# An mLSTM cell in sub-chunks of 64 tokens, and a new order of the first chunk's steps

## The chip, the cores and the metric

The kernel runs on one core of one Trainium2 chip. The metric is the device time of one execution in microseconds (us). Three timed runs of the kernel before gave 483.16, 483.56 and 483.63; the median is 483.56. A core has five engines with a queue of instructions each, executed in the order of the program: PE (TensorE, the matrix products), DVE (VectorE), ACT (ScalarE), POOL (GpSimd) and SP (SyncE, which here only issues DMAs). An instruction waits at the head of its queue until what it reads is there and what it overwrites has been read; nothing behind it on that engine starts before. PE's weight loads (PEld in the profile) run ahead of its products.

## The reference

The first half is an mLSTM cell over q, k, v of 4 batches, 8 heads, 768 tokens and 40 features, with gates per token:

```python
for t in range(S):
    m_new = np.maximum(f_gate[:, :, t] + m, i_gate[:, :, t])
    f_stab = np.exp(f_gate[:, :, t] + m - m_new)
    i_stab = np.exp(i_gate[:, :, t] - m_new)
    m = m_new
    C = f_stab * C + i_stab * outer(vt, kt)      # 40 x 40 per head
    n = f_stab * n + i_stab * kt
    h_tilde = C @ qt
    y[:, :, t] = sigmoid(o_gate[:, :, t]) * h_tilde / max(abs(n . qt), 1)
```

The second half is a feed-forward block on y, seen as 3072 tokens of 320 features: `gelu(y @ w_in) @ w_out`, with w_in 320x2048 and w_out 2048x320, both given in 64-bit floats.

## The kernel before, in words

**Chunks.** The 768 tokens are cut into six chunks (c = 0 to 5) of 128 tokens. A chunk of all four batches is 512 tokens for the feed-forward block. Inside a chunk the recurrence is written as products: the scores `k q^T` times a matrix of weights W (an exp of gate sums, masked so that a token sees only earlier ones), times the values; plus what q reads from the state that the chunk began with (`far`, scaled by gT). After that the state (40 by 41 for each head; column 41 is n) is decayed by `dec` and grown by `k^T (v * ewT)`.

**Cell steps.** Class `Cell` has a method for each step. The order of the work is written out by hand in two strings, FRONT and DOWN; each letter is a step and `play` emits the instructions of all engines for the letters in that order. Small letters in FRONT are chunk 0's cell, capital ones chunk 1's: m/M mask on POOL (`mask`, L407), w/W weights (`weights`: eight exps on ACT for a batch, L433; for chunk 0 PE writes the gate sums into PSUM first, L428 and L430), g/G sigmoid of the output gate on ACT (L439), t/T turning q and k on PE (L482, with two copies on ACT, L485), s/S scores (`scores`, L508, a product with W on DVE), c/C `carry` (state products on PE, L546, the read of the state, L551, and the state's update on DVE), v/V values (`values`, L622), y/Y `finish` (five operations on DVE, L635 to L640), x/X turning y on PE (L657, copied by ACT into first_x or x_hi), R splitting x on DVE (L675, L676). From chunk 2 on the batches go in pairs: `scores_two` (L524), `read_two` (L579), `update_two` (L590), and the second batch of each pair has the two halves of its 128 tokens swapped when loaded, so that all four 64 by 64 quarters of the PE array can be used at once.

**The front.** Chunk 0's cell needs the gates' running sums and maxima on DVE (L252 to L259, for chunk 0, chunk 1 by E, chunks 2 to 5 by N) and their exps on ACT. Beside it the weights are converted from 64-bit bits in 26 pieces: ten of w_in (512 elements a partition; two pieces of 128 rows for every 256 columns of a half, and one that holds the remaining 64 rows for 512 of them) and sixteen of w_out (320 elements). The letter P or the step J fetches a piece into one of four buffers. The letter K (`conv_one`) is for the next piece: two operations on DVE (L358, L363), two on ACT that make its power of two (L360, L361), and one on DVE (L365). The letter J (`conv_two`) is for the next piece not yet finished: two on DVE (L372, L375), the first of which needs ACT's power; then it fetches the piece four further on. So piece n is ready after the n-th J.

The chunk 0 feed-forward runs in plain f32. A is an up-step on the first half of the 512 tokens, U on the second; there are four of each, and the k-th uses two pieces of w_in with the one of remaining rows: the first needs pieces 1 to 3, the second 4 and 5, the third 6 to 8, the fourth 9 and 10. Two that follow each other (`U U`) are put out as one. Each issues its products on PE (L762, L768) and then its two gelus on ACT (L772). F is one of sixteen rows of the down product (L869, 8 instructions on PE), each with its own piece of w_out. While chunk 0's feed-forward runs, chunk 1's cell is computed.

**The later stages.** For c = 1 to 5, `up` gives chunk c's up-projection in split precision (L817, L828, gelus L832), then the string DOWN mixes chunk c's down-projection (14 products, letter F, L892) with the cell of chunk c+1.

**Queues.** SP issues all loads and stores in program order. Its loads of q, k, v and the gates for a batch are issued as one DMA each, or two where the halves are swapped. M, the running maxima, goes to memory and is read back spread over all partitions (L178).

Of the kernel before, what the change touches and what calls it, by code (L numbers as in the profile page):

```python
# [16 lines left out]
P = 128  # L17
# [11 lines left out]
    I2 O0 g0 L0 P0 L1 E k1 t0 P1 P2 k7 w0 N k2 w1 O1 K L2 Q s0 O3 w2 q D k2 d P3 t1 w3 c0 L3 J v0 t2 K K y0 s1 I7 v1  # L29
    I8 O2 J g1 L4 I5 c1 K I1 I2 y1 s2 x0 t3 B4 O4 B5 g2 J x1 s3 v2 c2 L5 y2 H T0 x2 G0 v3 g3 c3 K y3 M1 J L6 J A x3  # L30
    M0 K W0 O7 K A O6 O5 J M2 W1 S0 C0 K J J T1 U U K L7 V0 K T2 r J J A G2 K G1 Y0 W2 S1 K M3 C1 A J S2 J K W3 K V1 C2
    Y1 T3 J J U U S3 V2 K K J G3 J Y2 C3 X0 K V3 J K F J F K K B8 F J K F F J K F F F R0 X1 J J K F J F K X2 F J K F
    J Y3 K F R1 J F Z B9 B10 F X3 R2 Z R3 F p"""
DOWN = """
    M0 Z M1 W0 F L3 F B3 W1 Z Z S0 K2 C0 F h0 M2 G0 G1 G2 G3 V0 V1 W2 F Q2 K3 Q3 Y0 M3 D3 F F N W3 F S2 F C2 h2 V2 V3 j F Y1
    X0 R0 Y2 F F X1 Z Y3 R1 F X2 R2 F X3 R3 F"""
# [3 lines left out]
def kernel(  # L40
# [35 lines left out]
    NW = 3  # L76
# [25 lines left out]
    ewT = const.tile([P, NCH - 1, BH], F32, name="ewT")  # L102
    gT = const.tile([P, NCH - 1, BH], F32, name="gT")
    dec = const.tile([P, NCH - 1, B * NP], F32, name="dec")
    state = [const.tile([P, NP, 2 * D1], F32, name=f"state{b}") for b in range(B)]
# [6 lines left out]
    W = {n: shared([P, H, L], F32, f"W{n}") for n in range(B - 1)}  # L112
# [6 lines left out]
    last = gates.tile([P, P], F32, name="last")  # L119
    eye = gates.tile([P, P], BF16, name="eye")  # L120
    beyond = gates.tile([P, L], BF16, name="beyond")
    f_sb = gates.tile([BH, NCH, L], F32, name="f_sb")
    i_sb = gates.tile([BH, NCH, L], F32, name="i_sb")
    M_d = dram.tile([NCH - 1, BH, L], F32, name="M_d")
    swapped_d = [dram.tile([P, n, BH], F32, name=f"swapped{n}") for n in (NCH - 2, NCH - 3)]
# [5 lines left out]
    quarters = tuple(slice(R // 2 * n, R // 2 * (n + 1)) for n in range(4))  # L131

    def swapped(c, b):

        return c > 1 and b % 2 == 1

    def load(n, first=0, end=4):

        if n >= NCH * B:
            return  # L140
        c, b = divmod(n, B)
        for src, dst in ((q, qb), (k, kb), (v, vb), (o_gate, None))[first:end]:
            if dst and swapped(c, b):
                x, to = src[b, :, c * L:(c + 1) * L, :].rearrange("h p d -> p h d"), dst[turn_of(n)][:, :, 0:D]
                for i in range(2):
                    nc.sync.dma_start(out=to[halves[i]], in_=x[halves[1 - i]])
                continue
            nc.sync.dma_start(out=dst[turn_of(n)][:, :, 0:D] if dst else out_of(n),
                              in_=src[b, :, c * L:(c + 1) * L, :].rearrange("h p d -> p h d"))
# [17 lines left out]
    def load_M(n, to=None):  # L167

        if not B <= n < NCH * B:
            return  # L170
        c, b = divmod(n, B)
        src = M_d[c - 1, b * H:(b + 1) * H, :]
        if to is not None:
            Mb[n] = to
            nc.sync.dma_start(out=to, in_=src.unsqueeze(0).to_broadcast([P, H, L]))
            return
        Mb[n] = shared([P, H, L], F32, "W") if n // 2 == NW else wts.tile([P, H, L], F32, name="W", tag="W")
        nc.sync.dma_start(out=Mb[n].rearrange("p h l -> p (h l)"),  # L178
                      in_=src.rearrange("h l -> (h l)").unsqueeze(0).to_broadcast([P, H * L]))
# [8 lines left out]
    nc.gpsimd.memset(last, 0.0)  # L188
# [6 lines left out]
    for t in state:  # L195
        nc.gpsimd.memset(t, 0.0)
# [196 lines left out]
    class Cell:  # L393
# [16 lines left out]
        def weights(self, b):  # L410
# [23 lines left out]
            if n in (B, B + 1):  # L434
                load_M(n + 2)
# [579 lines left out]
```

## Time and profile before

| | |
|---|---|
| median of three timed runs | 483.56 us |
| span of the profiled execution | 487.5 us |
| its own time beside the span | none given beyond the span; it is 3.9 us over the median |
| PE busy | 474.4 us, 97% of the span |
| DVE, ACT, POOL busy | 351.2, 222.7, 72.0 us |
| first up-step of chunk 0 on PE (L762) | starts at 44.24 us |
| first product of chunk 1's feed-forward (L817) | starts at 133.4 us in the chain that ended last |
| first product of chunk 2's and of chunk 3's | 206.8 and 279.5 us |
| mean granted TensorE clock | 0.986 |

A row of the timeline gives start, duration, engine, line, operation, and out<-in by the program's tile names; f32 products appear as two records each. Products are pipelined, so the time that one group costs PE is read from its start to the start of the next group, not from the durations, which overlap. In brackets stands how long the engine was idle before the row and what ended that. "Busy" on PE is therefore an upper reading.

### The profile page before, as it was taken

The numbers are of one execution on the slowest core, as the hardware profiler recorded it, in microseconds if no ns is written. First come the engines' busy times: TensorE is split into PE (matmuls) and PEld (weight loads), VectorE is DVE, ScalarE is ACT, GpSimd is POOL, SyncE is SP. The second block draws the span as 40 slices with busy tenths as digits, with TensorE's granted clock in tenths as the row PEclk, the third lists the DMA queues.
The fourth block names the chain that finished last, engine by engine and source line by source line (L and its number), as shares of the span: only waits on it lengthen the run. The fifth ranks groups of instructions, "written<-read, shape, count | busy, mean of one in ns | idle before, by whom it ended". The sixth has DMA issues, their size and how long they took to land.

```text
span 487.5 us, 13234 instructions
## 1 busy us (share of the span) xinstructions
PE 474.4 (97%) x5380; PEld 411.0 (84%) x5380; DVE 351.2 (72%) x762; ACT 222.7 (46%) x477; POOL 72.0 (15%) x104
## 2 busy tenths in 40 slices
PE   8999999999999999999999999989999999999997
PEld 7787788877777898977898977889987898977997
DVE  7699879798879979855599756569755599724321
ACT  6786999954433852104852103852104672113300
POOL 3002120000020125400234200213300024000000
PEclk9699999999999999999999999989999999999999
DMA  9997986268431239551356541355561241000001
GB/s 175 193 171 172 199 194 148 69 168 204 125 59 13 34 71 192 83 111 14 41 107 162 79 103 16 37 94 127 108 123 19 30 78 24 28 28 0 1 1 54
DMA packets 170428, 44.57 MB, mean 91 GB/s; under 512 B 156448, under 2 KB 163904, under 8 KB 170368
## 3 DMA queue, kind: packets, MB, share of 16 engines
q1 hardware_dynamic: 170368, 43.73, 45.5%
q8 instruction: 42, 0.69, 0.6%
q14 instruction: 18, 0.15, 0.1%
HBM read 39.58 MB, written 4.13 MB: 90 GB/s over the span
## 4 chain that ended last, share of the span: by engine, by line
PE 70%; issue 13%; DVE 9%; POOL 2%; ACT 2%; SPq 2%; DMA 1%; DVEq 0%; POOLq 0%; ACTq 0%
PE po L892 23%; PE pu L817 16%; PE po L869 7%; PE pu L762 5%; PE pu L828 4%; PE ph L622 3%; PE ps L508 2%; SPq L158 1%; PE pu L768 1%; PE px L657 1%; PE ps L524 1%; PE pt L482 1%; POOL g L407 1%; DMA g<-M_d 1%; PE pf L590 1%
## 5 line engine op out<-in xcount | busy, mean ns | idle before, releaser
L892 PE MATMUL po<-w_out,g 128*128 128x160 f32 x640 | 91.6, 300 | 0.0
L892 PEld LDWEIGHTS po<-w_out,g 128*128 128x128 f32 x640 | 87.7, 190 | 2.1 <-ACT g L832 1.8
L832 ACT ACTIVATE g<-pu 128x512 f32<-128x512 f32 x80 | 40.8, 614 | 53.0 <-PE pu L828 52.8
L892 PE MATMUL po<-w_sums,sums 128*128 128x160 f32 x320 | 49.9, 310 | 1.9 <-issue 1.9
L892 PEld LDWEIGHTS po<-w_sums,sums 128*128 128x128 f32 x320 | 45.9, 196 | 3.1 <-issue 2.4
L817 PE MATMUL pu<-x_hi,w_in_hi 128*128 128x512 f32 x160 | 41.7, 402 | 0.0
L817 PE MATMUL pu<-x_lo,w_in_lo 128*128 128x512 f32 x160 | 40.6, 395 | 0.0
L667 ACT ACTIVATE x_hi<-px 128x384 fp32r<-128x384 f32 x20 | 9.8, 489 | 67.3 <-PE px L657 67.3
L433 ACT ACTIVATE W<-W,aT 128x128 f32<-128x128 f32 x128 | 39.2, 390 | 0.1
L817 PEld LDWEIGHTS pu<-x_hi,w_in_hi 128*128 128x128 f32 x160 | 28.5, 188 | 9.3 <-ACT g L832 4.1
L817 PEld LDWEIGHTS pu<-x_lo,w_in_lo 128*128 128x128 f32 x160 | 30.1, 188 | 7.2
L749 DVE TENSOR_TENSOR sums<-g 128x512 f32<-128x512 f32 x20 | 13.7, 687 | 30.8 <-ACT g L832 30.8
L869 PE MATMUL po<-w_out,g 128*128 128x320 f32 x128 | 35.2, 433 | 0.0
L869 PEld LDWEIGHTS po<-w_out,g 128*128 128x128 f32 x128 | 24.0, 190 | 9.6
L817 PE MATMUL pu<-x_all,w_mid 128*128 128x512 f32 x80 | 31.6, 395 | 0.0
L832 ACT ACT_TABLE_LOAD x5 | 6.4, 1283 | 55.1 <-PE pu L828 41.3
L817 PE MATMUL pu<-x_all,w_in_mid 128*128 128x512 f32 x80 | 31.6, 395 | 0.0
L721 DVE TENSOR_TENSOR w_in_mid<-w_in_hi,w_in_lo 128x512 fp32r<-128x512 f32 x20 | 13.8, 688 | 24.4 <-PE pu L817 24.4
L905 DVE TENSOR_TENSOR o_sb<-po,o_sb 128x320 f32<-128x320 f32 (+1 forms) x27 | 12.5, 463 | 25.7 <-PE po L892 21.7
L445 POOL MEMSET g<- 32x1024 f32 x8 | 7.6, 945 | 151.2 <-ACT W L433 125.6
L762 PE MATMUL pu<-first_x,w_in 128*128 128x256 f32 x128 | 29.2, 382 | 0.6 <-DVE w_in L375 0.6
L407 POOL TENSOR_SCALAR_AFFINE_SELECT W<-W 128x1024 f32<-128x1024 f32 (+2 forms) x20 | 20.9, 1056 | 59.6 <-DMA W<-M_d 51.6
(183 smaller groups left out, 915.5 us busy)
## 6 DMA issues: line engine op xcount, KB each, us to landing
W<-M_d SPq DMA_DIRECT2D x16, 512.0 KB, 5.6
bits<-in_moe_w_in_dram SPq DMA_DIRECT2D x20, 256.0 KB, 4.7
bits<-in_moe_w_out_dram SPq DMA_DIRECT2D x16, 320.0 KB, 3.2
ob<-in_o_gate_dram SPq DMA_DIRECT2D x24, 160.0 KB, 3.6
out_dram<-o_sb SPq DMA_DIRECT2D x24, 160.0 KB, 1.9
vb<-in_v_dram SPq DMA_DIRECT2D x14, 160.0 KB, 5.0
kb<-in_k_dram SPq DMA_DIRECT2D x14, 160.0 KB, 5.1
g<-M_d SPq DMA_DIRECT2D x4, 512.0 KB, 4.4
```

The source lines that it names most:

```text
L407: nc.gpsimd.affine_select(out=x, in_=x, compare_op=OP.is_ge, fill=1.0e30, base=base, pattern=[[0, H], [1, x.shape[2]]], channel_multiplier=-1)
L433: nc.scalar.activation(out=W[n][:, h, :], in_=src, func=AF.Exp, scale=-1.0, bias=aT[:, self.c, r:r + 1])
L622: nc.tensor.matmul(ph[r, h, :], Pm[:, h, r], vb[turn_of(n)][:, h, :], start=True, stop=True)
L721: nc.vector.tensor_tensor(out=w_mid[i], in0=w_hi[i], in1=w_lo[i], op=OP.add)
L749: nc.vector.tensor_tensor(out=s1, in0=a21, in1=a22, op=OP.add)
L762: nc.tensor.matmul(banks[-1][e][:, i - i0, :], in_tile(i, x)[:, e, i % 2 * P:(i % 2 + 1) * P], first_x[:, x, t0:t1], start=(x == 0 and i = ...
L817: nc.tensor.matmul(pus[i][e], w[k][:, e, i * P:(i + 1) * P], x[:, k, :], start=(n == 0 and k == 0), stop=False, skip_group_check=True)
L828: nc.tensor.matmul(pu[e], w[r, i // 2, i % 2 * P:(i % 2 + 1) * P], x[r, NX, :], start=False, stop=(n == 2), skip_group_check=True)
L832: nc.scalar.activation(out=g.t[:, HF * e + i, :], in_=pu[e], func=AF.Gelu, scale=4097.0)
L869: nc.tensor.matmul(po[b], g.t[:, f, b * L:(b + 1) * L], w_out[:, f, :], start=(f == 0), stop=(f == NF - 1))
L892: nc.tensor.matmul(bank[at][:, i, :], lhs(j, t), rhs(j), start=(first and i == 0 and j == 0), stop=(i == n - 1 and j == HF - 1), skip_grou ...
L905: nc.vector.tensor_tensor(out=to, in0=pb, in1=x, op=OP.add)
```

## The change: what it does

The cell is rewritten so that every product of it uses 64 rows by 64 columns of the PE array, for a pair of batches u (0 or 1) at a time. A chunk falls into two sub-chunks j of 64 tokens. A tile of tokens now holds sub-chunk j of the two batches of pair u in its two halves of 64 partitions (so gates are loaded and results stored in two DMAs of 64 rows each, L141 and L801 of the new file). Scores and values reach only within a sub-chunk; the state is read, decayed and grown twice in a chunk. W for a pair of batches has the size that it had for one batch, so the exps are half as wide; M is spread per pair in two DMAs of 64 partitions. The swapped loads, their round trip through memory, and the separate forms for later chunks go away. Chunks 0 and 1 use the same form as the others.

New letters: z `weigh_values`, r `read`, a `decayed`, b `grown` (in chunk 1: Q, e, h), with the pair or batch and the sub-chunk as numbers; D and d now take a range of chunks. N, the gates of chunks 2 to 5, moves from early in FRONT to between the seventh and the eighth J; the loads, conversions and up-steps are ordered anew.

```diff
 FRONT = """
-    I2 O0 g0 L0 P0 L1 E k1 t0 P1 P2 k7 w0 N k2 w1 O1 K L2 Q s0 O3 w2 q D k2 d P3 t1 w3 c0 L3 J v0 t2 K K y0 s1 I7 v1
-    I8 O2 J g1 L4 I5 c1 K I1 I2 y1 s2 x0 t3 B4 O4 B5 g2 J x1 s3 v2 c2 L5 y2 H T0 x2 G0 v3 g3 c3 K y3 M1 J L6 J A x3
-    M0 K W0 O7 K A O6 O5 J M2 W1 S0 C0 K J J T1 U U K L7 V0 K T2 r J J A G2 K G1 Y0 W2 S1 K M3 C1 A J S2 J K W3 K V1 C2
-    Y1 T3 J J U U S3 V2 K K J G3 J Y2 C3 X0 K V3 J K F J F K K B8 F J K F F J K F F F R0 X1 J J K F J F K X2 F J K F
-    J Y3 K F R1 J F Z B9 B10 F X3 R2 Z R3 F p"""
+    I2 L0 L1 P0 O0 P1 O1 k1 t0 P2 w0 E t1 K w1 L2 D0,1 L3 z0 J d0,1 z1 s0 K c0 b0,0 a0,1 b0,1 r0,1 O2 g0 g1 v0 J O3 K y0 P3 t2
+    w2 y1 x0 x1 J t3 w3 A K s1 z2 z3 J c1 b1,0 a1,1 b1,1 K r1,1 g2 g3 v1 J A y2 K y3 x2 x3 J U U B2 L4 K L5 J N O4 K O5 J B3 A
+    D1,2 U d1,2 T0 M0 K J D2,6 L6 W0 T1 K M1 J d2,6 H W1 A L7 U S0 Q0,0 e0,0 C0 K O6 h0,0 J O7 e0,1 Q0,1 h0,1 K G0 G1 V0 J F Y0 K
+    T2 J F Y1 K X0 J W2 F K T3 J F R0 K X1 J F W3 K J F R1 S1 Q1,0 e1,0 K J C1 F h1,0 e1,1 K Q1,1 h1,1 J F G2 G3 V1 K J F Y2 K J
+    F Y3 K J F K X2 J F K J F R2 X3 K J F Z K J F R3 Z K J F Z F F"""
 DOWN = """
-    M0 Z M1 W0 F L3 F B3 W1 Z Z S0 K2 C0 F h0 M2 G0 G1 G2 G3 V0 V1 W2 F Q2 K3 Q3 Y0 M3 D3 F F N W3 F S2 F C2 h2 V2 V3 j F Y1
-    X0 R0 Y2 F F X1 Z Y3 R1 F X2 R2 F X3 R3 F"""
+    M0 M1 a0,0 a1,0 Z W0 W1 Z r0,0 F L3 F Z C0 b0,0 a0,1 F S0 Z r0,1 b0,1 G0 K2 G1 F G2 G3 V0 W2 K3 F Q2 W3 Y0 Q3 F Y1 r1,0 N F C1 b1,0 a1,1 X0
+    R0 S1 F r1,1 b1,1 j X1 F V1 R1 F Y2 F Y3 F X2 R2 F X3 R3 F"""
...
-    state = [const.tile([P, NP, 2 * D1], F32, name=f"state{b}") for b in range(B)]
+    state = [[const.tile([P, 2, NP, D1], F32, name=f"state{u}{j}") for j in range(2)] for u in range(B // 2)]
...
+        def scores(self, u):
...
             kT, qT = [self.kT.pop(b) for b in two_b], [self.qT[b] for b in two_b]
+            ps = [ps_tr.tile([P, 2, NP, R], F32, name="ps", tag="tr") for hip in range(2)]
...
+            for i in range(2):
+                for p in range(NP):
+                    for t in halves:
                         for hip in range(2):
                             r = halves[hip]
-                            nc.tensor.matmul(ps[i][hip][halves[x ^ i], p, t], kT[i][r, p, halves[x]], qT[i][r, p, t],
-                                             start=True, stop=True)
+                            nc.tensor.matmul(ps[hip][t, i, p, :], kT[i][r, p, t], qT[i][r, p, t], start=True, stop=True)
+            for hip in range(2):
+                w = W[2 * c + u].rearrange("p i (m two) t -> p (i m) two t", two=2)[:, :, hip, :]
+                nc.vector.tensor_tensor(out=w, in0=ps[hip].rearrange("p i m t -> p (i m) t"), in1=w, op=OP.mult)
+
+        def read(self, u, j):
...
+            for p in range(NP):
+                for i, b in enumerate(two_b):
+                    for hip in range(2):
+                        r = halves[hip]
+                        nc.tensor.matmul(self.banks[u][hip][halves[i], j, p, :], self.qT[b][r, p, halves[j]], state[u][j][r, i, p, :],
+                                         start=True, stop=True)
...
+            for hip in range(2):
+                nc.vector.tensor_tensor(out=by_hip(far, hip), in0=self.banks[u][hip][:, j],
+                                        in1=by_hip(decay, hip).to_broadcast([P, NP, D1]), op=OP.mult)
+
+        def decayed(self, u, j):
+
+            if (self.c > 0 or j == 1) and (self.c + 1 < NCH or j == 0):
...
+                self.engine.tensor_tensor(out=flat(state[u][1 - j]), in0=flat(state[u][j]), in1=d, op=OP.mult)
+
+        def update(self, u):
...
+            subs = range(2 if c + 1 < NCH else 1)
...
             for i, b in enumerate(two_b):
...
                 for p in range(NP):
                     for hip in range(2):
-                        nc.tensor.matmul(pc[halves[hip], p, :], kb[turn_of(n)][:, 2 * p + hip, :], vw[:, 2 * p + hip, :],
-                                         start=True, stop=True)
+                        for j in subs:
+                            s, h = halves[j], 2 * p + hip
+                            nc.tensor.matmul(self.pc[j][halves[hip], i, p, :], kb[turn_of(c * B + b)][s, h, :], vw[i][s, h, :],
+                                             start=True, stop=True)
+
+        def grown(self, u, j):
...
+        def values(self, u):
...
+            for h in range(H):
+                for i, b in enumerate(two_b):
+                    for j in range(2):
+                        s = halves[j]
+                        nc.tensor.matmul(ph[j][halves[i], h, :], Pm[s, i, h, :], vb[turn_of(c * B + b)][s, h, :], start=True, stop=True)
...
-    def send(c, b, o_sb):
-        nc.sync.dma_start(out=out[b * S + c * L:b * S + (c + 1) * L, :], in_=o_sb)
+    def send(c, n, o_sb):
+
+        u, j = divmod(n, 2)
+        for i in range(2):
+            t = (2 * u + i) * S + c * L + R * j
+            nc.sync.dma_start(out=out[t:t + R, :], in_=o_sb[halves[i]])
```

The decays of the gates are now one exp for each sub-chunk; their last values are spread to the partitions by one product with rows of ones (`decays_last`) after a product with a selector on DVE. The state has two tiles for a pair: sub-chunk 0 reads the first and writes the second, sub-chunk 1 the other way.

## The prediction

> **What bounds the kernel now.** I read the page (parts 1 and 2), then the timeline of PE, then those of DVE and ACT over the front, then PE's over one later stage.
>
> ```profile
> span 487.5 us, 13234 instructions
> ...
> PE 474.4 (97%) x5380; PEld 411.0 (84%) x5380; DVE 351.2 (72%) x762; ACT 222.7 (46%) x477; POOL 72.0 (15%) x104
> ...
> PEclk9699999999999999999999999989999999999999
> ```
>
> PE has work nearly always, and the clock fell only early (15.4 to 25.3 us, 0.50 in windows of 1 us) and once near 323. The kernel is PE's queue; what counts is its sum of work and its gaps. The front, on PE:
>
> ```profile
> 44.24 3.72 PE L762 MATMUL pu<-first_x,w_in 128*128 128x256 f32 x16
> 47.89 1.13 PE L768 MATMUL pu<-first_x,w_rest 64*128 64x256 f32 x8
> ...
> 50.81 3.29 PE L762 MATMUL pu<-first_x,w_in 128*128 128x256 f32 x14 [0.57 <-DVE w_in L375]
> ...
> 58.10 7.07 PE L762 MATMUL pu<-first_x,w_in 128*128 128x256 f32 x32
> 65.10 2.00 PE L768 MATMUL pu<-first_x,w_rest 64*128 64x256 f32 x16
> ```
>
> One up-step (A or U) is 4.45 us, a double one 8.85. From the first at 44.2 to chunk 1's products at 133.4 PE is dense (gaps of 1 us). It can be so because five pieces of w_in are converted (K, then J) before the first up-step, and the tenth at 73.6. A conversion on DVE and ACT:
>
> ```profile
> 23.09 0.69 DVE L372 SCALAR_TENSOR_TENSOR pow<-bits,pow 128x512 uint32<-128x512 uint32 x1
> 23.81 0.69 DVE L375 SCALAR_TENSOR_TENSOR w_in<-sig,pow 128x512 f32<-128x512 f32 x1
> 24.42 0.42 DVE L358 TENSOR_SCALAR pow<-bits 128x512 uint32<-128x512 uint32 x1
> 24.75 0.42 DVE L363 TENSOR_SCALAR sig<-bits 128x512 uint32<-128x512 uint32 x1
> 25.21 0.69 DVE L365 SCALAR_TENSOR_TENSOR sig<-bits,sig 128x512 f32<-128x512 uint32 x1
> ```
> ```profile
> 28.72 0.73 ACT L360 ACTIVATE pow<-pow,e_hi 128x512 f32<-128x512 uint32 x1
> 29.49 0.72 ACT L361 ACTIVATE pow<-pow,e_lo 128x512 uint32<-128x512 f32 x1
> 67.53 2.07 ACT L772 ACTIVATE g<-pu 128x512 f32<-128x512 f32 x4
> ```
>
> J costs 1.33 (first start to next start), K 1.40; for a w_out piece 0.95 and 0.98. Between them lie 1.46 on ACT, in ACT's order: behind any gelu (L772, 0.5 each) put there earlier, which waits for its up-step. Last, a later stage (chunk 3's cell inside chunk 2's products), and the slow spot:
>
> ```profile
> 241.28 1.09 PE L579 MATMUL pf<-state,qT 64*64 64x41 f32 x64
> 242.31 2.44 PE L892 MATMUL po<-w_sums,sums 128*128 128x160 f32 x16
> 244.68 1.13 PE L590 MATMUL pf<-vw,kb 128*64 128x41 f32 x32
> 245.74 1.67 PE L622 MATMUL ph<-vb,W 128*32 128x41 f32 x128
> ...
> 320.22 0.40 PE L892 MATMUL po<-w_sums,sums 128*128 128x160 f32 x1
> 322.22 3.98 PE L892 MATMUL po<-w_sums,sums 128*128 128x160 f32 x15 [1.59 <-issue]
> ```
>
> Starts give the cost on PE: reads 1.03, update 1.06, values 1.60 for a pair of batches. After 1.59 idle the clock stood at 0.50 for 3.4 us: 1.7 lost.
>
> **Stages 1 to 4: the cell.** For a pair the old cell takes scores 1.39 and 1.49, reads 1.03 and 1.07, updates 1.06 twice, values 1.60 and 1.85: 10.55 a chunk. New: reads, updates and values are each 64 records of 64x64, 41 columns, as L579 has them: 1.05 each. Scores are 64 records of 64 columns; below them lies the read row (1.05), above them the old row (1.49, half its records twice as wide); I take 1.25, halfway. That is 4.4 a pair, 8.8 a chunk: -1.75. A switch of form costs: 16 records alone between small ones take 2.37, inside a run 2.18, so 0.2, and the new order has ten such insertions for eight: +0.4. Three chunks at -1.35, and the last, which had no update (8.43) and now has half of one (7.75 + 0.4): -0.3. Sum -4.35; bounds -8 (scores at the low end, no dearer switches, the four waits for DVE's L530, 1.1 in all, gone) and +1 (scores as now, switches doubled).
>
> A read of the second sub-chunk waits for the state to be grown on DVE; one down-product (2.2) and the scores (1.25) lie between against 0.41, so nothing; if DVE is behind by more, everything behind that read on PE waits, up to 1 a stage. By the trace a read record takes 16.1 ns (1.03 over 64). The Trainium skill, TensorE: Matmul & The Clock Gate, section Back-to-back issue gap, gives a matmul of 1 to 64 columns a floor of about 25 ns; the row disagrees. At 25 ns the three kinds would cost 1.65 more a pair, an estimate from that page, and the sum below would end 13 higher.
>
> Costed at nothing in the stages: ACT's exps of half the width (at most 1.8 less a chunk; ACT is idle for half of each stage); DVE's eight score products becoming two; POOL's masks (four of 1.1 a chunk) and decays (twice 128x328, 0.83 at most by the vw row), under the up-projections' 28 us; M's loads of half the bytes, and on SP 24 more gate issues and 24 more output issues of 0.4, beside transfers with slack. The last output issues twice: +0.4. If POOL's cover goes, the first read waits for nothing, the second for the decay: 0.8.
>
> **The front: the first up-step comes sooner.** SP sends q and k of batches 0 and 1 ahead of v and the gates, and only pair 0's cell stands before A. DVE: gates to 6.6 as now, 1.3 of small new operations, chunk 1's gates 1.35 and decays; ACT does the copies of batch 0, eight exps, the copies of batch 1, then K1's pair, to 14.2; J1 15.6. Scores of pair 0 run at half clock as PE does then now, products 20.2; J2 near 26; two finishings of 1.69 each; J3 31.8. Batch 3's turn and masks on PE: first A at 33.5 (31 to 36) against 44.2.
>
> **But each conversion then hangs on PE.** I follow the new order over the engines. A to 38.0; scores 39.2; two products on DVE 40.5; weighted values 41.4; J4 42.7; state 44.0; K5 45.4; read-outs 46.3; J5 47.6. The second A needs pieces 4 and 5: to 52.1. Its gelus (53.3) stand on ACT ahead of K6's pair (54.7) and of first_x (55.7), for which the double U waits: to 64.5. Its four gelus stand ahead of K7's pair: 66.0, 67.4; J7 68.7. Then N, the gates of chunks 2 to 5, moved here from 8.6: 5.7 on DVE (74.4), its exps (75.5), K8's pair (77.0), J8 78.3. The third A needs piece 8 for its last 1.0: 79.3. U 84.1, gelus 85.2, copies 86.2, K9's pair 87.6, a table load, eight exps and two copies (4.3), K10's pair 93.4, J10 94.7. Only now the fourth A and U: 103.6, and chunk 1's scores 104.9. Behind these DVE has 16 w_out conversions of 1.93 (30.9) and the rest of the cell: 2.5 products, 1.9 read-outs, 3.3 state, 1.7 sums, 6.6 finishing, 0.8 values, 2.9 splits and 0.6 of a weight, 51.2: J26 at 156.1. The last down-row follows: 158.3. PE has 46 of work from 104.9, so DVE ends last. The front grows by 158.3 - 133.4 = 24.9. Bounds: 141 (DVE's rows end to end, no wait) and 166 (0.1 for each of some forty hand-overs, and DVE idle for another 4).
>
> PE is idle over 1.59 before the second A (2.7), the double U (3.6), U (4) and the fourth A (7): up to four half clocks, 6.8; I count one, 1.7, after the longest. In the Trainium skill, TensorE: Matmul & The Clock Gate, the section on HAM oscillation, a gap must exceed some 3 us to halve the clock. The trace shows 1.59 to be enough; by the rule three of the gaps count, and the sum would be 3.4 higher.
>
> **Sum** against the profiled span of 487.5 (0.8% over the median of the timed runs, 483.56; the difference is the same for both kernels, as far as the trace can tell): +24.9 + 1.7 - 4.35 + 0.4 = +22.65. On the median: 506.2, say 506.
>
> **Rivals.**
> *The conversions keep ahead of PE* (the other side). DVE's rows up to J8 sum to 47, so J8 could stand near 51 were nothing waited for; then PE is dense from 33.5 and ends its 91 us of work (today's 89.2 from 44.2 on, pair 1's first cell and the gates' transposes added, the narrower products taken off) at 124.5: -8.9 - 4.35 + 0.4, 470.7. It decides from a front end before 137.3. For it: DVE is 18% idle in the first 100 us today. Against it: the order of ACT, where K7's pair is behind the double U.
> *The first half of the chain is shorter*: J5 at 38, full clocks: -9.6 and -1.7: 495.
> *More half clocks and waits*: four bursts at half clock (+5.1) and the upper bound's 7.7 in part: 514.
> *The small products are no cheaper than they were*: update and value records at the 33 ns of L590 instead of 16.4 give 2.1 a pair, 16 over the stages: 522. The change would then not do what it says. Against it: L579.
>
> **How the numbers follow.** Main case 0.52 (own range 499 to 512); short chain 0.18; more half clocks 0.18; dear products 0.05; conversions ahead 0.07. The range 491 to 517 leaves out the last two and thin tails. A measurement here tells 0.2% (1 us) from nothing: faster 0.08 (the rival and some of the short chain's tail), same 0.02, slower 0.90.
>
> **What would show it.** The first first_x product at 31 to 36; PE idle for over 5 us between the double U and the third up-step, and again before the fourth; J10 beyond 88; chunk 1's w_in_hi products from 150 to 166; a later stage, 72.6 now (206.8 to 279.5), at 70.5 to 72.5; values 1.05 a pair. I am wrong if ACT's pairs don't wait for gelus, so that PE stays dense after 40, or if a stage shrinks by over 4.

## The result and the profile after

The changed kernel takes 573.31 us (median of four runs, 570.97 to 575.91) where the kernel before takes 483.6: a ratio of 1.184, 95% interval 1.180 to 1.188. The forecast was 506 (491 to 517): slower was right, and the loss is four times the one forecast. The profiled execution of after took 570.97, with a span of 569.1.

From the page of after, its span, the busy time of the engines and the granted TensorE clock in 40 slices of the span:

```profile
span 569.1 us, 13273 instructions
...
PE 494.7 (87%) x5404; PEld 419.0 (74%) x5404; DVE 344.5 (61%) x732; ACT 208.4 (37%) x469; POOL 74.0 (13%) x97
...
PEclk9676977778999998999999999999999997899999
```

DVE's work fell from 351.2 to 344.5 and ACT's from 222.7 to 208.4, so no engine got more to do than it can carry. PE is busy for 20 us more, but its records lengthen with the clock, and the clock's row now stands at 6 to 8 in most slices of the first 140 us, where it stood at 9 from the third slice on. PE waits, and runs slowly after it has waited.

The first product of the feed-forward of chunks 1 to 5 cuts the span into the front, four stages with a cell in them, and a last one without:

| us | front | stage 1 | 2 | 3 | 4 | last |
|---|---|---|---|---|---|---|
| before | 133.0 | 73.5 | 72.9 | 75.2 | 70.2 | 62.6 |
| after | 187.0 | 79.3 | 78.6 | 78.5 | 82.3 | 63.4 |
| forecast of the change (front: 24.9 + 1.7) | +26.6 | together | | | -4.35 | +0.4 |
| measured | +54.0 | together | | | +26.9 | +0.8 |

So both large terms missed, the front by 27 us and the stages by 31.

The front of after on PE. Columns as in the prediction's rows; the bracket is PE's idle time before the row and what ended it:

```profile
34.98 3.62 PE L700 MATMUL pu<-first_x,w_in 128*128 128x256 f32 x16
...
49.77 5.99 PE L700 MATMUL pu<-first_x,w_in 128*128 128x256 f32 x14 [0.79 <-DVE w_in L365]
...
60.10 7.17 PE L700 MATMUL pu<-first_x,w_in 128*128 128x256 f32 x32 [1.40 <-ACT first_x L600]
...
75.14 0.63 PE L226 MATMUL pg<-ident,a 32*128 32x32 f32 x4 [5.93 <-DVE a L234]
75.70 5.42 PE L700 MATMUL pu<-first_x,w_in 128*128 128x256 f32 x16
...
101.68 0.76 PE L273 MATMUL pd<-spread,half_rows 32*128 32x128 f32 x2 [5.55 <-DVE spread L270]
102.37 5.73 PE L700 MATMUL pu<-first_x,w_in 128*128 128x256 f32 x16
...
122.80 4.46 PE L811 MATMUL po<-w_out,g 128*128 128x320 f32 x8
...
169.62 2.42 PE L811 MATMUL po<-w_out,g 128*128 128x320 f32 x8 [3.61 <-DVE w_out L365]
```

The up-steps start at 35.0, 47.8, 60.1, 75.7 and 102.4; the forecast had 33.5, 47.6 and 55.7, for the third an end at 79.3 (measured 83.7), and 94.7. Three of them run at half clock, wholly or in part (the granted clock was 0.50 from 45.0 to 55.3 us, for one): 16 records take 3.72 at full clock, and the third and fourth up-step took 5.42 and 5.73; the 14 records that took 3.29 before took 5.99. DVE, over the front: group (line, operation, shapes, count), busy us and mean ns, then idle us before the group and what ended it; and the longest of these waits:

```profile
L362 DVE SCALAR_TENSOR_TENSOR pow<-bits,pow 128x320 uint32<-128x320 uint32 (+1 forms) x26 | 15.6, 602 | 24.0 <-ACT pow L351 23.9
```
```profile
71.83 0.69 DVE L362 SCALAR_TENSOR_TENSOR pow<-bits,pow 128x512 uint32<-128x512 uint32 x1 [9.68 <-ACT pow L351]
```

L362 opens the second half of a conversion (J) and needs the power of two from ACT. In after, 23.9 us of DVE's front go to waiting for it.

One later stage of after, chunk 3's cell in chunk 2's products, on PE:

```profile
296.91 0.67 PE L499 MATMUL pf<-state,qT 64*64 64x41 f32 x30 [1.30 <-ACT g L770]
297.51 6.29 PE L834 MATMUL po<-w_out,g 128*128 128x160 f32 x32
303.73 1.14 PE L535 MATMUL pc<-vw,kb 64*64 64x41 f32 x64
...
307.17 1.16 PE L485 MATMUL ps<-qT,kT 64*64 64x64 f32 x64
...
311.08 1.14 PE L557 MATMUL ph<-vb,W 64*64 64x41 f32 x64
312.15 4.61 PE L834 MATMUL po<-w_out,g 128*128 128x160 f32 x32
318.47 0.31 PE L499 MATMUL pf<-state,qT 64*64 64x41 f32 x2 [1.46 <-DVE qT L437]
319.21 0.66 PE L499 MATMUL pf<-state,qT 64*64 64x41 f32 x26 [0.43 <-DVE qT L437]
...
325.58 1.15 PE L485 MATMUL ps<-qT,kT 64*64 64x64 f32 x62 [1.53 <-DVE x_all L614]
```

The products themselves cost what was forecast: update 1.07 (303.73 to 304.80), values 1.07, scores 0.98. Around them stand three waits that the stage of before does not have, and 32 records of the down-projection that take 6.22 behind the first of them, where 32 take 4.54 elsewhere. From start to start the four cost 1.64, 2.54, 1.96 and 1.68, 7.8 in all.

### The profile page after: what moved, and what is told of

The parts are those of the page before. It is cut to its first block, busy times and chain, and to the rows that moved or that the text cites. A ratio compares the mean times of both kernels' runs of the same rounds, so it can differ in the third digit from the quotient of the medians.

```text
span 569.1 us, 13273 instructions
## 1 busy us (share of the span) xinstructions
PE 494.7 (87%) x5404; PEld 419.0 (74%) x5404; DVE 344.5 (61%) x732; ACT 208.4 (37%) x469; POOL 74.0 (13%) x97
## 4 chain that ended last, share of the span: by engine, by line
PE 63%; DVE 17%; ACT 10%; issue 3%; DMA 3%; SPq 3%; DVEq 0%; ACTq 0%
PE po L834 25%; PE pu L755 15%; PE pu L700 5%; PE pu L766 3%; PE ph L557 3%; PE ps L485 2%; ACT W L419 2%; SPq L150 2%; PE pf L499 2%; DVE pow L362 2%; ACT pow L350 2%; ACT pow L351 2%; DVE kT L437 2%; DVE qT L437 2%; ACT g L770 1%
## 5 line engine op out<-in xcount | busy, mean ns | idle before, releaser
L834 PE MATMUL po<-w_out,g 128*128 128x160 f32 x640 | 94.7, 308 | 0.0
L834 PEld LDWEIGHTS po<-w_out,g 128*128 128x128 f32 x640 | 90.8, 196 | 1.0 <-ACT g L770 0.4
L770 ACT ACTIVATE g<-pu 128x512 f32<-128x512 f32 x80 | 40.8, 614 | 52.9 <-PE pu L766 52.8
L811 PE MATMUL po<-w_out,g 128*128 128x320 f32 x128 | 41.4, 472 | 7.6 <-DVE w_out L365 7.6
L488 DVE TENSOR_TENSOR W<-ps,W 128x512 f32<-128x512 f32 x24 | 15.5, 686 | 40.9 <-PE ps L485 40.9
L811 PEld LDWEIGHTS po<-w_out,g 128*128 128x128 f32 x128 | 25.1, 206 | 19.7 <-DVE w_out L365 10.4
L419 ACT ACTIVATE W<-W,aT 128x64 f32<-128x64 f32 x160 | 39.5, 334 | 0.1
L700 PE MATMUL pu<-first_x,w_in 128*128 128x256 f32 x128 | 36.6, 449 | 2.2 <-ACT first_x L600 1.4
L499 PE MATMUL pf<-state,qT 64*64 64x41 f32 x704 | 19.3, 237 | 19.5 <-DVE qT L437 8.9
L396 POOL TENSOR_SCALAR_AFFINE_SELECT W<-W 64x1024 f32<-64x1024 f32 x20 | 26.2, 1311 | 72.5 <-DMA W<-M_d 71.6
L700 PEld LDWEIGHTS pu<-first_x,w_in 128*128 128x128 f32 x128 | 28.6, 229 | 8.6 <-ACT first_x L600 1.6
L499 PEld LDWEIGHTS pf<-state,qT 64*64 64x64 f32 x704 | 15.5, 143 | 25.0 <-DVE qT L437 9.9
L687 DVE TENSOR_TENSOR sums<-g 128x512 f32<-128x512 f32 x20 | 13.7, 687 | 31.1 <-ACT g L770 31.1
L350 ACT ACTIVATE pow<-pow,e_hi 128x320 f32<-128x320 uint32 (+1 forms) x26 | 16.2, 624 | 44.4 <-DVE pow L348 44.3
```

The costliest lines, as they stand in the source:

```text
L350: nc.scalar.activation(out=p, in_=pu, func=AF.Relu, scale=-I23, bias=e_hi)
L396: nc.gpsimd.affine_select(out=Mb[2 * self.c + u][r], in_=Mb[2 * self.c + u][r], compare_op=OP.is_ge, fill=1.0e30, base=0, pattern=[[0, 2], ...
L419: nc.scalar.activation(out=W[n][:, i, h, :], in_=src[:, h, :], func=AF.Exp, scale=-1.0, bias=aT[:, self.c, r:r + 1])
L499: nc.tensor.matmul(self.banks[u][hip][halves[i], j, p, :], self.qT[b][r, p, halves[j]], state[u][j][r, i, p, :], start=True, stop=True)
L700: nc.tensor.matmul(banks[-1][e][:, i - i0, :], in_tile(i, x)[:, e, i % 2 * P:(i % 2 + 1) * P], first_x[:, x, t0:t1], start=(x == 0 and i = ...
L770: nc.scalar.activation(out=g.t[:, HF * e + i, :], in_=pu[e], func=AF.Gelu, scale=4097.0)
```

## The experiments

No kernel here leaves out work. All of them, the kernel before too, run some idle products on PE, whose result nobody reads; how many is said below, under the clock. Times are medians; ratios are to the kernel before, run on the same chip, with 95% intervals.

### One wait of the stage, then all three

The first theory: the three waits make the stages' loss. `r0,0`, the first read, stood directly behind the up-projection, whose last gelu (L770) frees the PSUM banks that the read writes. `Q3` stood on DVE behind batch 0's finishing. `S1` needed a PSUM bank that R0's split (L614) frees, and R0 stood behind N. The first run moves only the read behind a row of down-products:

```diff
-    ... Z W0 W1 Z r0,0 F L3 F Z C0 ...
+    ... Z W0 W1 Z F r0,0 L3 F Z C0 ...
```

> Only the first read of a stage (r0,0) is put behind the first down-row in DOWN. Theory 'waits': it then finds its two PSUM banks free, since the gelus that it waited for (1.30 of idle, 1.64 from start to start) end under that row's 2.27 us; the half clock that followed it in two of the stages (1.7 each) goes too. Stages 1 to 4 shrink by 1.6 each, and two of them by 1.7 more: about -10, 573 to 563. Theory 'dear switches' (the loss lies in the small products between the down-rows, wherever they stand): nothing changes, 573, or it gets 1 slower, since one more switch of form is paid in each stage.

Measured: 567.18 us, 1.170 (1.151 to 1.189), which is not clear of the 1.180 to 1.188 of after. The wait is gone, and stages 1 to 3 are as long as before the edit (79.9, 78.6, 78.5); only stage 4 went from 82.3 to 77.6. The same stretch of PE's timeline, chunk 3's cell:

```profile
318.63 0.31 PE L499 MATMUL pf<-state,qT 64*64 64x41 f32 x2 [1.47 <-DVE qT L437]
319.37 0.66 PE L499 MATMUL pf<-state,qT 64*64 64x41 f32 x26 [0.43 <-DVE qT L437]
319.96 4.11 PE L834 MATMUL po<-w_sums,sums 128*128 128x160 f32 x16
...
327.53 1.98 PE L485 MATMUL ps<-qT,kT 64*64 64x64 f32 x62 [1.66 <-DVE x_all L614]
```

The half clock now stands behind the next waits: the 16 records at 319.96 took 4.03 to the next start, where they took 2.37, and the 62 scores 1.91 for 1.08. Over the four stages the clock was at 0.50 for 20.5 us in both kernels. So waits in one stage can't be priced one by one: here the slow spell behind the first came back behind the next when the first was gone.

All three, with Q3 moved ahead of Y0, the second read behind a row, and R0 ahead of that row's products:

```diff
-    ... Q2 W3 Y0 Q3 F Y1 r1,0 N F C1 b1,0 a1,1 X0 R0 S1 F r1,1 b1,1 j X1 F V1 ...
+    ... Q2 Q3 W3 Y0 F Y1 F r1,0 N C1 b1,0 a1,1 X0 R0 F S1 r1,1 b1,1 j F X1 V1 ...
```

> Three moves in DOWN: the first read behind a down-row; the transposes Q3 up to Q2 and the read r1,0 behind a further down-row; the down-row after the second scores moved ahead of them, so that the split of x (R0) frees their PSUM bank meanwhile. Theory 'waits': of the 7.8 us that chunk 2's stage loses from start to start (1.64, 2.54 and 1.96 in the three waits, 1.68 at half clock) nearly all goes; four stages of 78.6 to 82.3 come to 71 to 72.5 each, -31 in all, 573 to 542; the front stays at 187. Theory 'dear products or switches': a stage stays above 76.

Measured: 558.77, 1.152 (1.138 to 1.167), half the gain. PE's waits in chunk 2's stage, then the row of POOL that ends the first:

```profile
319.92 0.68 PE L535 MATMUL pc<-vw,kb 64*64 64x41 f32 x32 [1.18 <-POOL vw L471]
321.80 0.64 PE L595 MATMUL px<-ident,ob 128*128 128x128 f32 x2 [1.20 <-DVE ob L578]
327.49 1.10 PE L485 MATMUL ps<-qT,kT 64*64 64x64 f32 x59 [1.04 <-DVE x_all L614]
```
```profile
319.13 0.74 POOL L471 TENSOR_TENSOR vw<-vb,ewT 128x328 f32<-128x328 f32 x1 [13.13 <-DMA vb<-in_v_dram]
319.82 1.57 POOL L573 TENSOR_TENSOR ob<-far,ob 128x320 f32<-128x320 f32 x2
```

The edit made new waits. Q3 weighs batch 3's values on POOL, for which vb had not landed; POOL stood for 13.13 us, and the two finishings behind it (L573) with it, for which DVE and then PE's px waited. In its old place, behind Y0, Q3 lets the finishing pass. And N's sums on DVE (L864, 2.35) still stood ahead of R0. The next version leaves Q3 where it was, puts a row ahead of the second read, and N behind R0:

```diff
-    ... Q2 W3 Y0 Q3 F Y1 r1,0 N F C1 b1,0 a1,1 X0 R0 S1 F r1,1 b1,1 j X1 F V1 ...
+    ... Q2 W3 Y0 Q3 F Y1 F r1,0 C1 b1,0 a1,1 X0 R0 F S1 r1,1 b1,1 N j F X1 V1 ...
```

> DOWN again, other moves than in s_all, where the weighing of the last values came to stand ahead of two finishings in POOL's queue, and the subtraction N ahead of the split R0 in DVE's: r0,0 behind the first down-row; r1,0 behind one more down-row, with Q3 left behind Y0; the second scores behind the next down-row, and N behind them. Theory 'waits': the three waits go and no other takes their place; stages 1 to 3 come from 79.3, 78.6, 78.5 to 71 to 73, the fourth from 82.3 to 69 to 71; about -32, 573 to 541. Theory 'DVE is the bound there' (it was busy for 9.2 of the 10 us from 315 to 325): what is moved away comes back as another wait, and the stages stay above 75.

Measured: 543.04, 1.121 (1.115 to 1.128): 30.3 less than after, and 2 over the 541 expected. The stages are 73.6, 70.7, 71.2, 71.4 and PE's only waits of over 0.25 from 190 us to the end are 1.77 and 0.43 in stage 1 and 0.43 in stage 4. The clock's row on its page:

```profile
PEclk9676879597898999999999999999999999999999
```

The sum of the stages is 286.9, after 318.7 in the kernel changed as it was. The forecast's sum was 287.4 (291.8 of before less 4.35). So the stages' miss was these waits and the half clocks behind them.

### The front: one K

The order of before does K for the next piece ahead of the J of the last, so ACT's pair (1.46) runs beside DVE's work; the new order puts each K directly ahead of its own J. One more K after the third J, and nothing else, restores the distance for all pieces behind it:

```diff
-    ... x0 x1 J t3 w3 ...
+    ... x0 x1 J K t3 w3 ...
```

> Only one more K is put into FRONT, after the third J, so that from the fourth piece on each conversion's first half runs one piece ahead of its second half and ACT's two operations lie under another piece's work. Theory 'no piece ahead': DVE no longer stands for ACT's pair (23.9 us in the sixteen waits at L362, 9.7 of it before J7): J8 comes about 8 sooner, and a piece of w_out takes 1.93 instead of 3.07 where nothing lies between its K and J; chunk 1's first product moves from 187 to about 168 (160 to 175), 573 to 554. Theory 'PE and its clock': the front is held by PE's half clocks and PE's own waits for the cell; then under 5 is won. The stages stay as they are.

Measured: 555.2, 1.145 (1.130 to 1.160); chunk 1's products start at 166.2 instead of 187.0. The group over the front, in this run:

```profile
L362 DVE SCALAR_TENSOR_TENSOR pow<-bits,pow 128x320 uint32<-128x320 uint32 (+1 forms) x26 | 16.1, 618 | 0.3 <-ACT pow L351 0.3
```

The 23.9 us of waits are 0.3, and the fourth up-step starts at 88.3 instead of 102.4. By the medians one letter is worth 18.1 us; the profiled front gained 20.8, and the stages of this execution took 3.9 more (322.6 for 318.7), with more of them at half clock.

Both edits together (this K, and the stages of the second run above):

> Both edits at once. Theory: they lie in different parts of the span and add up: about -50, 523 (515 to 530). Rival: a front that ends earlier meets something of the stages (loads of chunk 2, the split of the weights), and the sum falls short by 5 or more.

Measured: 542.49, 1.119 (1.105 to 1.133). The K is worth 16.3 beside s_all's 558.77, so the two add up; the total fell short of the expectation as s_all had. Its front has the order of f_k, instruction by instruction, and ended at 173.7 instead of 166.2.

N, the gates of chunks 2 to 5, stood between two conversions. f_k with N ahead of the first up-step:

```diff
-    ... J N O4 K O5 J ...
+    ... J O4 K O5 J ...
-    ... t3 w3 A K s1 ...
+    ... t3 w3 N A K s1 ...
```

> The front of f_k, and N (the gates of chunks 2 to 5, 5.9 us on DVE) moved from between J7 and J8 to before the first up-step, where DVE stands for 7.8 us for the scores behind that up-step. Theory: there it costs nothing, and in f_k's chain J8 comes 5 sooner; but PE waits for J8 for only 0.7 in f_k, so the gain is small, 0 to 4 from 555: what is moved was not the cause of the long front, the missing piece ahead was. Rival 'N is the gap': -5 or more against f_k.

Measured: 553.45, 1.143 (1.128 to 1.158), front 171.6: no gain that stands out of the two fronts of one order above. So N's place isn't shown to be a cause.

### The clock

Between 30 us and the end of its front the mean granted clock of after is 0.85, which is 46 us at 0.50; in the kernel before it is 1.00. One part of the change that bears on this is nowhere priced: the kernel before runs 80 records of idle products on PE up to 34.3 us (most of them by the letters k and I of FRONT), and the new order keeps 30 of them. No run here puts just those back. The next one is f_k with 104 records of idle products more (the letter k) at nine of its waits; the diff shows the seven up to the double up-step:

```diff
-    ... y1 x0 x1 J K t3 ... J c1 b1,0 a1,1 b1,1 K r1,1 ... J A y2 K y3 x2 x3 J U U ...
+    ... y1 k8 x0 k8 x1 J K t3 ... J k7 c1 b1,0 a1,1 b1,1 K k3 r1,1 ... J k3 A y2 K y3 k2 x2 x3 J k5 U U ...
```

> The front of f_k with idle products (k, whose result is never read) put into nine of PE's waits of 0.7 to 2.5 us, as many as fill each wait at full clock. Theory 'the clock': the waits themselves are due to DVE and ACT and stay, but the half clocks that follow them in f_k (first A, second A 6.0 for 3.3, fourth A 5.9 for 3.7, values, the first F: about 8 us) go, and with them the scatter of the front's end (166 and 174 for the same order in two kernels): chunk 1 starts at 157 to 163, and the stages stay at 78 to 82. Rival 'the half clock costs nothing since DVE is the bound': chunk 1 starts at 165 or later.

Measured: 549.06, 1.130 (1.112 to 1.149), front 162.6. The clock of its page, and its second up-step:

```profile
PEclk9599998799899998899997899998999996999999
```
```profile
49.68 3.29 PE L700 MATMUL pu<-first_x,w_in 128*128 128x256 f32 x14 [0.80 <-DVE w_in L365]
```

Work added to PE keeps the clock up: behind a wait as long as before (0.80 for 0.79), with the longer waits ahead of it filled, the second up-step's 14 records are back at 3.29, and from 30 us to the end of the front 14 us are at half clock where f_k has 32. What this is worth in time is less sure. The medians differ by 6.1 us and the profiled fronts by 3.6, but the intervals of the two runs overlap (two executions each), and two fronts of one order differ by 7.5. The prediction had counted one half clock (1.7); the front of after held at least the four that its rows show (2.7, 1.7 and 2.0 on the up-steps, and the first row of the down product, 4.46 at 122.80 for 2.32).

### Other orders of the front

With s_two's stages, three orders of the new cell's front. The first keeps the new order, with K ahead, N early, weighted values ahead of scores, and conversions further ahead (the diff shows the string's first part):

```diff
-    ... x0 x1 J t3 w3 A K s1 z2 z3 J ... y2 K y3 x2 x3 J U U B2 L4 K L5 J N O4 K O5 J B3 A D1,2 U ...
+    ... x0 x1 J K t3 w3 N A K z2 z3 s1 J ... y2 K y3 J K x2 x3 J U U B2 L4 K L5 J O4 O5 B3 A K D1,2 J U ...
```

> Front: one piece ahead, N in DVE's hole before the first up-step, z2 z3 ahead of s1, the sixth and seventh J ahead of x2 and the double up-step, the last turn of chunk 1 (T3) ahead of W2's exps, the state's growth ahead of the next conversion. Stages: as s_two. Theory: DVE's work has no long wait left, so PE is dense from the first up-step at 34 to 36; with 92 to 95 us of work to chunk 1's first product that starts at 130 to 140, and with stages of 71 to 73 the whole comes to 480 to 492, near the kernel before. Rival 'DVE is full': the F rows of chunk 0 go on waiting for w_out, and chunk 1 starts after 150, 505 or more.

Measured: 517.68, 1.069 (1.060 to 1.078); front 163.8, stages 72.8, 71.6, 71.8, 71.0. The rival's number: the stages keep their gain, the front doesn't come near that of before.

The second computes the whole of chunk 0's cell and converts five pieces before the first up-step, as the order of before does:

```diff
-    ... t3 w3 A K s1 z2 z3 J c1 ... J A y2 K y3 x2 x3 J U U ...
+    ... t3 w3 y0 z2 z3 s1 M0 y1 J K x0 x1 c1 ... W0 W1 A J K N A J K J K U U ...
```

> The new cell in the old kernel's order of the front: both pairs of chunk 0 first, five conversions done before the first up-step, one piece ahead, chunk 1's first pair between the up-steps; stages as in s_two (71 to 73). Theory: the loss of the front lies in the new order (an up-step before pair 1's cell, no piece ahead), not in the 64-row products: the first up-step comes at 44 to 50, and chunk 1 starts at 130 to 142; with stages of 73, 71, 71, 71 and 63.5 the end is at 480 to 492, equal to the kernel before within 2%. Rival: the new cell's chain of steps is itself longer (two state updates in a row, both batches before any product): chunk 1 starts after 150.

Measured: 515.3, 1.061 (1.045 to 1.076). The first up-step came at 57.5 and the front ended at 161.2, on the rival's side again. The third lies between the two, with up-steps from 39.8, conversions always one ahead and 20 more records of idle products up to 14 us (the letters k2 and k8, outside the part shown):

```diff
-    ... t3 w3 A K s1 z2 z3 J c1 ... J A y2 K y3 x2 x3 J U U ...
+    ... g2 g3 y1 K J z2 z3 s1 x1 c1 M0 b1,0 a1,1 b1,1 J K A ... J K y2 y3 J K A M1 x2 x3 J K W0 W1 J K U U ...
```

> Front of the new cell in a third order, drawn from the waits of best1 and old_order: scores and update of pair 1 ahead of the first up-step (DVE waited 3.0 for them behind it), W of all four batches made in one stretch on ACT, the finishings of pair 1 ahead of the second up-step's wait, nine conversions and chunk 1's W before the double up-step's gelus, chunk 1's first pair between the later up-steps. Stages as s_two. Theory: DVE's work (110 us before, 116 here) leaves room for a front as short as the old one if no engine's head waits long; the double up-step starts at 48 to 54 instead of 64.3, and chunk 1 at 132 to 145: 482 to 497. Rival: the new cell's front can't be made short by order: above 150.

Measured: 508.86, 1.048 (1.041 to 1.055); front 156.3, once more the rival's. Some of the waits that hold PE in these two fronts, first old_order, then best2:

```profile
31.80 2.46 PE L485 MATMUL ps<-qT,kT 64*64 64x64 f32 x64 [2.41 <-ACT kT L461]
38.13 0.66 PE L595 MATMUL px<-ident,ob 128*128 128x128 f32 x2 [3.02 <-DVE ob L578]
40.79 0.47 PE L595 MATMUL px<-ident,y_rest 128*128 128x128 f32 x1 [2.00 <-DVE y_rest L584]
```
```profile
27.11 1.97 PE L458 MATMUL pt<-ident,qk 128*128 128x128 f32 x8 [3.73 <-ACT kT L461]
37.19 1.09 PE L535 MATMUL pc<-vw,kb 64*64 64x41 f32 x32 [4.76 <-DVE vw L471]
61.54 0.69 PE L595 MATMUL px<-ident,ob 128*128 128x128 f32 x2 [5.41 <-ACT g L710]
```

The orders move the waits to other engines; none of the three takes them away.

### The old cell in front, the new one behind

Chunks 0 and 1 in the cell and the order of before (chunk 1 writes its state in the new layout; without the swapped loads' letters r, p, B10), chunks 2 to 5 in sub-chunks with s_two's string:

```diff
-        cell = Cell(c)
+        cell = Cell(c) if c < 2 else SubCell(c)
```

> The new cell for chunks 2 to 5 alone, with the stages' order of s_two; chunks 0 and 1 keep the old cell, and the front the old order (without the halves' round trip through memory and one load of M; the new decays of chunks 2 to 5 made in it). Theory: the loss was the front's order and three misplaced waits a stage, and the 64-row products are cheaper by what the prediction summed: the front ends at 131 to 136 as before, stages 1 to 4 take 72 to 74, 71, 71 and 70.5 against 73.5, 72.9, 75.2 (one 1.59 gap in it) and 70.2, and the profiled span is 481 to 486 against 487.5, 0.3 to 1.2% faster than the kernel before. Rival: the new cell needs the new front's data flow or costs DVE and POOL so much that the stages stay above 73.5: same or slower than before.

Measured: 488.08 beside 484.52, 1.0047 (1.0017 to 1.0078). Front 134.7, stages 71.9, 70.8, 72.6, 70.5. So the front of before is still to be had, with the new cell behind it, but the gain that was expected did not come: it is slower by 0.2 to 0.8%. Its last px, at 131.81, waited 2.20. DVE's split L722, which frees its bank, ended at 131.67 (the profile's bracket names an ACT operation that ended at 131.68), and the theory for the next run is that DVE was late because POOL masked chunk 2's weights beside it. DVE, then POOL:

```profile
117.37 1.31 DVE L410 SCALAR_TENSOR_TENSOR sig<-bits,sig 128x320 f32<-128x320 uint32 x1
118.60 1.42 DVE L417 SCALAR_TENSOR_TENSOR pow<-bits,pow 128x320 uint32<-128x320 uint32 x1
120.06 0.49 DVE L420 SCALAR_TENSOR_TENSOR w_out<-sig,pow 128x320 f32<-128x320 f32 x1
```
```profile
117.11 2.58 POOL L737 TENSOR_SCALAR_AFFINE_SELECT W<-W 64x1024 f32<-64x1024 f32 x2
```

The last run fetches those weights at the front's end, so that the masks run in chunk 1's up-projection:

```diff
-    ... J K F J F K K B8 F J K F ... R1 J F Z B9 F X3 R2 Z R3 F
+    ... J K F J F K K F J K F ... R1 J F Z F X3 R2 Z R3 B8 B9 F
```

> The mixed version (chunks 0 and 1 in the cell and the order of the kernel before; chunks 2 to 5 in sub-chunks, with the reads behind a down product) with chunk 2's weights fetched at the end of the front, so that POOL's two pairs of masks run in chunk 1's up-projection and not beside DVE's last conversions. Theory: DVE operations slow down while POOL's masks run (L410 took 1.31 instead of 0.49, L417 1.42, L683 1.11, L686 1.08 in the mixed version), some 3.7 in all, which put the last turned y 2.2 late on PE. Then the front ends 1.5 to 2.5 sooner, near 132.5 to 133, and the time is 0.3 to 0.5% under the mixed version's 488.08 beside 484.52: a ratio to the kernel before of 0.999 to 1.002. Rival: the four DMAs land later and stage 1 waits for the weights or DVE's splits of chunk 1's own weights are slowed instead: ratio 1.004 to 1.01 again. In either case a later stage stays at 70.5 to 72.6.

Measured: 484.1 (12 runs) beside 485.33 (17 runs), 0.9982 (0.9955 to 1.0008). The masks ran at 134.6, these rows of DVE stood at 0.49 again and PE had no wait from 110 us to the end of the front, at 130.7. In the up-projection the masks slow DVE's operations on the weights (L1000 1.51 and 1.62 for 0.69), for which PE does not wait. Stages 72.6, 70.9, 70.8, 70.5. The page of its profiled execution, the fastest of the twelve (481.2):

```profile
span 479.2 us, 12719 instructions
...
PE 468.7 (98%) x5153; PEld 404.8 (84%) x5153; DVE 339.2 (71%) x720; ACT 215.1 (45%) x477; POOL 79.5 (17%) x102
...
PEclk9899999999999999999999999999999999999999
```

The interval reaches over 1, so this version isn't shown to beat the kernel before; it takes at most 0.1% more, with PE's work 5.7 us less than in the profile of before.

## Why the prediction was wrong

By the medians 67 us were missed: 31 in the stages, 27 in the front, 6 in the step from the span to the median, and some 2 by which the median of after lies over its profiled execution.

**Right: the direction, and the front up to the second up-step.** The first up-step came at 35.0 (forecast 31 to 36), PE was idle for 5.93 and 5.55 before the third and the fourth, and ACT's pairs did wait for gelus (J7 could start at 71.8; forecast 67.4). The products of updates and values cost 1.07, the two halves of a read 0.56 to 0.61 each, and the scores 0.98 to 1.08, taken at 1.25.

**Wrong: "so nothing", with at most "up to 1 a stage", and "Costed at nothing in the stages".** The new order was given no wait of PE in the stages, and they took 31 us more than forecast. The second sub-chunk's read was looked at for the state it reads; the waits came from elsewhere, from what stands ahead in a queue: a PSUM bank freed by the last gelu, a transposed q behind a finishing on DVE, a PSUM bank held by a split that stands behind N. With them gone, the sum of the stages is the forecast's (286.9 and 287.4). Some 3.3 of the 291.8 from which that was worked out are the gap and the half clock in stage 3 of before; without these it would have been 284.1, and the last run, whose stages hold one wait of 1.11 and one of 0.28, has 284.8.

**Wrong: 16 conversions of 1.93, with DVE's work "end to end".** 1.93 is the price with K a piece ahead. With K directly ahead of J, ACT's pair stands in series: a w_out piece then takes 2.47 (170.94 to 173.41) where ACT is free, and more where its pair stands behind exps or copies (the longest such wait was 3.40). The walk over the engines had this wait for K6 to K10 and dropped it for w_out. From chunk 1's first scores to the end of the front took 72 us where 53.4 were forecast: 14.8 of DVE idle, 9.1 of them this wait, and 57.4 of work for 51.2 (5.1 of it in eight operations that ran longer than their kind elsewhere, all beside work on POOL). The rest of the front's miss, 10, lay ahead of these scores (114.8 for 104.9). The one K takes 17 to 21 us off the profiled front (187.0 to 166.2, and 190.6 to 173.7 beside s_all) and 16 to 18 off the time.

**Mis-sized: the half clocks.** One was counted, 1.7, and four called possible. The four rows named above lost 8.5 of PE's time, and f_clk's idle products took 18 us of half clock out of f_k's front. That the new order drops 50 records of idle products was not weighed. The clock was down before the second up-step began (0.50 from 45.0 on), behind waits of 1.96 and 0.91 that ended at 42.71 and 44.77. The rule weighed in the prediction (the Trainium skill, TensorE: Matmul & The Clock Gate, on HAM oscillation), by which only gaps of some 3 us count, doesn't describe these rows; a section of the same page, A second HAM failure mode: psum-queue depth-cycling, has the clock falling where PE is idle often and briefly, and with that the rows of the front agree; the single wait of 1.30 in the stage fits neither.

**Mis-sized: the step from the span to the median.** The sum took the 3.9 between the profiled span and the median off for both kernels. The executions run here took 1.8 to 2.1 more than their span, so the profiled execution of before took some 489.4, 5.8 over its median, 3.3 of it the slow spot in stage 3. Had all terms of the change been right, the span would have been 510.15. best1, with both mended, has 514.5: front 163.8 for 160.0, stages 287.2 for 287.4, last 63.5 for 63.0. Of the 11.7 between its median and the 506, 4.35 are of the span, 5.7 are this step, and the rest is its median over its profiled execution.

**The rivals.** "More half clocks and waits" is what happened, and it cost far more than the 8 us it was priced at. "Dear products" did not happen: at full clock 64 records of L535 or L557 cost 1.07 and of L499 some 1.2, near L579's 1.03 and far from that rival's 2.1. "Conversions ahead" needs the K that f_k adds, and even with it no front of the new cell ended before 156; its point of decision was 137.3.

**What stays open.** The new cell's front, in its best order, ends 22 to 26 us later than the front of the two mixed versions (156.3 against 134.7 and 130.7). DVE's work is nearly the same (115.9 us busy in the front of old_order, 110.7 in that of before), so that work isn't it. PE is idle for 30.7 us of old_order's front, against 5.5 in before, and from 30 us on its clock was at 0.50 for 34 us (best2: 26), where before and the mixed versions have none. Whether the longer chain of a batch (two state updates one after the other, two batches before any product) does it, or that no good order was found, or in part that these fronts hold 30 or 50 records of idle products and not 80, isn't settled: the cell, the order and the idle products were changed together.

## What to carry to other kernels

When work moves to another place in a hand-written order, look up for each product not only what it reads but which PSUM bank it writes and who frees it last, and for each engine what now stands ahead in its queue; the cheaper products were worth 4 us, and three overlooked waits with the half clocks behind them cost 31. Keep a two-engine operation (here K on ACT, J on DVE) one item ahead: a single letter was worth 16 to 18 us. Take waits out together and look at the next ones, since with one wait removed alone the slow clock stood behind the next, and nothing was gained in three stages of four.

## What the runs showed of the hardware

**The clock falls after short waits, and not always the same way.** In after the granted clock was 0.50 from 45.0 to 55.3 us behind waits of 1.96 and 0.91 (14 records took 5.99 for 3.29), and from 297.6 to 301.0 behind one of 1.30 (6.22 for 4.54). Yet a wait of 1.77 in s_two (at 243.66) and one of 2.20 in the mixed version (at 131.81) brought no half clock. Apart from those that the end of a span cuts off, a spell at 0.50 lasted a whole multiple of 3.4 us in these traces, from 3.4 up to 27.3 (old_order, 31.1 to 58.4). One front, in the same order, ended at 166.2 and at 173.7 in two kernels that differ only in their later stages, with 32 and 44 us at half clock from 30 us on.

**POOL and DVE hinder each other.** In the mixed version, DVE operations with two operands in SBUF took 1.31 and 1.42 instead of 0.49 while two masks of 1.3 ran on POOL: one of them for each mask. In after, the same happened (L362 at 152.75):

```profile
152.75 1.42 DVE L362 SCALAR_TENSOR_TENSOR pow<-bits,pow 128x320 uint32<-128x320 uint32 x1
154.21 1.31 DVE L365 SCALAR_TENSOR_TENSOR w_out<-sig,pow 128x320 f32<-128x320 f32 x1
155.44 0.48 DVE L545 TENSOR_TENSOR state<-state,pc 128x328 f32<-128x328 f32 x1
```
```profile
152.44 2.74 POOL L396 TENSOR_SCALAR_AFFINE_SELECT W<-W 64x1024 f32<-64x1024 f32 x2
```

The Trainium skill, SBUF — State Buffer, section Who interferes with whom, describes a port pair that the two engines share and that one of them holds for a whole instruction, where DVE has two inputs in SBUF and POOL reads SBUF. The rows agree: while the two masks run (152.44 to 155.18), DVE gets one operation done for each, and at 155.44, with the masks over, it is back at its 0.48. The last run, which moved only the loads that start the masks, had 0.49 in those conversions and a front 3.9 us shorter.

**64 by 64 products of 41 columns** cost 16 to 17 ns a record in a run of 64 at full clock: 1.07 us for updates and for values in the stage of after shown above, and 1.03 for the reads in the kernel before. In two halves of 32 the reads took 0.56 to 0.61 each.
